# A four-sequence decode kernel: the first queries and scores of its second layer, one key head at a time

## The chip, the cores and the metric

The kernel runs on one core of a Trainium2 chip. The metric is the device time of one execution in microseconds; lower is better.

## What is computed

Two layers over four sequences (B = 4, one new token each, D = 512): attention over a cache of 4096 positions with 32 query heads on 8 key heads of width 128, and a gated feed-forward of width 1792. Both layers use the same weights and the same caches.

```
def _A_ref(x, k_cache, v_cache, wq, wo):
    q = (x @ wq) ...                      # 32 heads of 128
    k, v = repeat(k_cache, 4), repeat(v_cache, 4)
    p = softmax(q . k * Dh ** -0.5)
    return (p . v) @ wo
def _B_ref(x, w_gate, w_up, w_down):
    return (gelu(x @ w_gate) * (x @ w_up)) @ w_down
x = x + _A_ref(layernorm(x), ...)
x = x + _B_ref(layernorm(x), ...)
x = x + _A_ref(layernorm(x), ...)
x = x + _B_ref(layernorm(x), ...)
```

## The kernel before

The work goes sequence by sequence. A key or value head of one sequence is two tiles (`t` = 0 and `NT - 1` = 1, called "last") of 128x2048 bf16, 512 KB each. The keys of one sequence fill SBUF (`KP`, sixteen tiles); each is loaded once, turned in place by VectorE in 32x32 blocks (`Keys.turn`), and serves layer 1 and then layer 2. Values have eight slots (`slots`, `VRing`) and are mostly loaded once for each layer. Key heads stand in two groups of four, `gx` (first in layer 2) and `gy`.

The order of the work is written out by hand, and every engine runs its own instructions in that order. All loads but that of x are issued by SyncE's queue (SP), in the order written, and an issue waits until its target is free.

- `attend_first` does layer 1 of sequence 0, issues the loads of the weights (`load_rest`: wo, w_gate, w_up, and w_down in the parts of `WD_PARTS`), and moves two key tiles, heads 2 and 3 of `gy` at the last t, into four banks of PSUM (`Parked`), so that the first two key tiles of sequence 1 can be loaded into their place at once.
- `dense_first` is the feed-forward of layer 1 for sequence 0. `busy` issues matmuls whose result nobody reads, where TensorE waits for a load.
- Then come the queries of layer 2 for the group `gx`: 64 small matmuls (`q_proj`), rounding on VectorE (`q_round`), sums on TensorE (`q_sums`), and the mask on VectorE that lays them out as weights (`q_spread`, into `qb`).
- `attend(b + 1)` does layer 2 of sequence b together with layer 1 of sequence b + 1. It scores group `gx` (`scores`: for each of four parts `be`, one matmul of 512 columns for each of four heads side by side, in four column strips of the array), loads the keys of the next sequence as tiles come free, takes the softmax (`soft`: maximum, exponential on ScalarE; `soft_turn`), then the same for `gy`; the values of layer 2 follow (`vals2`), then two groups of scores and the values (`vals1`) of layer 1 of the next sequence, whose output goes to `dense`, where the rest of layer 2's values (`prev.fill`) are summed between the steps of the feed-forward.

In `attend`, for the first call alone, the two parked tiles are copied back by ScalarE in four pieces, two before and two after the first softmax:

```
for t in range(NT):
    scores(sc2[0], gx, t)
    if parked and t == 0:
        ...
        parked.back(home, 2)
        ...
        keys.load_pairs(GH // 2 - 1)
    else:
        keys.load_pairs(GH // 2)
before.whole()
p0 = soft(sc2[0], norm)
if parked:
    parked.back(home, 2)
q_build(qy())
```

## Time and profile before

| | |
|---|---|
| Median of three runs | 273.4 us (272.24 to 274.52) |
| Profiled execution | 271.11 us, span 269.2 us, mean granted TensorE clock 0.854 |
| Busy | TensorE 190.0 us, VectorE 174.7, ScalarE 64.2, GpSimd 2.7 |
| Loads | 103.08 MB, mean 383 GB/s |
| Key turns on VectorE (L488) | 64, 1.21 us each |
| Score matmuls (L531) | 512 of 512 columns, 0.45 us each, overlapping |
| Copies back from PSUM on ScalarE (L512, keys) | 4 of 128x1024, 1.01 us each |
| Park copies on VectorE (L500, keys) | 4 of 128x512 words, 0.68 us each, 55.2 to 57.0 us |

All times inside the execution count from the start of the span. In lists of instructions the columns are start, duration, engine, line, operation, what it writes and reads, shape and count; in brackets how long the engine was idle just before and what ended it. A merged row has the duration from its first start to its last end. In tables of stretches the columns are the stretch, its length, the busy time and count of TensorE's matmuls, TensorE's weight loads, VectorE, ScalarE and GpSimd, the granted TensorE clock (1 is full), the share of the DMA engines' time, and GB/s. Lines of the form L123 are those of the kernel before.

### The profile page before, as it was taken

What the parts mean: (1) busy time and instruction counts of PE and PEld (TensorE: products, weight loads), DVE (VectorE), ACT (ScalarE), POOL (GpSimd) and SP (SyncE); (2) the same over time, 40 slices, a digit from 0 to 9 for tenths busy, and PEclk for the clock granted to TensorE, in tenths of its full rate; (3) what the DMA queues carried; (4) which work ended last, traced back from release to release, by engine and by line L of the source; (5) the groups of instructions that cost most, each with busy time, mean ns of one, the idle gap of its engine ahead of it and who ended that gap; (6) DMA issues with size and microseconds to landing.
All of it is one profiled execution on the core that took longest, in us unless ns stands there. A gap on an engine that the chain in (4) does not pass through costs nothing.

```text
span 269.2 us, 8883 instructions
## 1 busy us (share of the span) xinstructions
PE 190.0 (71%) x3943; PEld 113.8 (42%) x3943; DVE 174.7 (65%) x428; ACT 64.2 (24%) x125; POOL 2.7 (1%) x8
## 2 busy tenths in 40 slices
PE   1395255634597896968869969687788786788893
PEld 1333133633364443544426335454354354453561
DVE  3394952130124799875676999566759995768863
ACT  1001000100404412030422610304137113044640
POOL 2000000000000000000000000000000000000001
PEclk9999559555599798687897997889979979799999
DMA  6999999999993999999999999999999999999940
GB/s 244 421 417 421 418 420 416 413 382 402 411 360 100 419 415 418 420 418 416 402 386 417 417 420 417 416 422 416 412 417 415 417 419 417 416 391 386 417 159 3
DMA packets 32430, 103.08 MB, mean 383 GB/s; under 512 B 2692, under 2 KB 8584, under 8 KB 32392
## 3 DMA queue, kind: packets, MB, share of 16 engines
q1 hardware_dynamic: 32368, 102.51, 95.1%
q8 instruction: 31, 0.51, 0.7%
q14 instruction: 7, 0.06, 0.1%
q10 hardware_dynamic: 24, 0.01, 0.0%
HBM read 102.50 MB, written 0.00 MB: 381 GB/s over the span
## 4 chain that ended last, share of the span: by engine, by line
DMA 51%; DVE 21%; PE 17%; SPq 6%; issue 2%; ACT 1%; DVEq 0%; ACTq 0%
DMA v_t<-in_A_v_cache_dram 29%; DMA kp<-in_A_k_cache_dram 13%; DVE kp L488 10%; PE sc L531 7%; DMA wu_sb<-in_B_w_up_dram 5%; DMA kp<-in_A_v_cache_dram 4%; SPq L142 4%; PE so L712 2%; DVE pe L541 2%; DVE q L280 2%; DVE qb L316 1%; PE ot L779 1%; PE y L246 1%; PE q L274 1%; SPq L143 1%
## 5 line engine op out<-in xcount | busy, mean ns | idle before, releaser
L488 DVE STREAM_TRANSPOSE kp<-kp 128x1024 f32<-128x1024 f32 x64 | 74.0, 1206 | 0.2 <-issue 0.2
L531 PE MATMUL sc<-kp,qb 128*32 128x512 bf16 x512 | 66.6, 449 | 7.5 <-DVE qb L316 2.5
L779 PE MATMUL ot<-pe,v_t 128*128 128x32 bf16 x1120 | 35.3, 181 | 14.4 <-DMA v_t<-in_A_v_cache_dram 12.4
L779 PEld LDWEIGHTS <-v_t 128*128 128x128 bf16 x1120 | 33.1, 99 | 24.2 <-DMA v_t<-in_A_v_cache_dram 15.9
L531 PEld LDWEIGHTS <-qb 128*32 128x32 bf16 x512 | 21.3, 102 | 42.2 <-issue 23.1
L553 ACT ACTIVATE pe<-sc,nl 128x512 bf16<-128x512 f32 x8 | 5.5, 687 | 84.9 <-DVE pe L550 67.2
L583 PE MATMUL x<-pe,ident_bf 128*32 128x128 bf16 x192 | 6.0, 255 | 15.1 <-DVE pe L561 15.0
L583 PEld LDWEIGHTS <-ident_bf 128*32 128x32 bf16 x256 | 5.6, 107 | 18.9 <-issue 17.1
L541 DVE TENSOR_REDUCE pe<-sc 128x1 f32<-128x512 f32 x12 | 8.3, 689 | 7.9 <-PE sc L531 7.9
L720 DVE STREAM_TRANSPOSE so<-so 128x256 f32<-128x256 f32 (+1 forms) x19 | 11.1, 584 | 3.2 <-PE so L712 3.1
L712 PE MATMUL so<-v_t,pe 128*32 128x256 bf16 x192 | 10.2, 341 | 2.8 <-ACT pe L586 1.4
L246 PE MATMUL y<-OT_bf,wo_sb 128*128 128x32 bf16 x192 | 7.3, 190 | 6.8 <-DMA wo_sb<-in_A_wo_dram 6.7
L246 PEld LDWEIGHTS <-wo_sb 128*128 128x128 bf16 x256 | 8.6, 102 | 8.0 <-DMA wo_sb<-in_A_wo_dram 7.1
L586 ACT CAST pe<-x 128x512 bf16<-128x512 f32 x12 | 7.0, 585 | 20.3 <-PE x L583 20.3
L712 PE MATMUL so<-v_t,pl 128*32 128x256 bf16 x192 | 9.7, 283 | 2.9 <-DMA v_t<-in_A_v_cache_dram 2.6
L379 DVE TENSOR_TENSOR xb<-XX,y 128x4 bf16<-128x4 f32 (+1 forms) x9 | 1.6, 173 | 14.2 <-PE y L246 14.1
L246 PE MATMUL q<-xb,wq_sb 128*128 128x5 bf16 (+1 forms) x192 | 5.4, 170 | 7.3 <-DMA wq_sb<-in_A_wq_dram 7.3
L561 DVE STREAM_TRANSPOSE pe<-pe 128x512 bf16<-128x512 bf16 x12 | 8.4, 697 | 3.2 <-ACT pe L553 3.2
L616 DVE TENSOR_TENSOR OT_bf<-ot,rden 128x8 bf16<-128x8 f32 (+1 forms) x20 | 3.0, 156 | 11.1 <-PE ot L779 11.0
L360 PE MATMUL yr<-wo_sb,OT_bf 128*2 128x512 bf16 (+1 forms) x96 | 10.2, 494 | 0.0
L310 PE MATMUL qe<-q_bf,ident_bf 128*32 128x16 bf16 x256 | 4.4, 175 | 8.2 <-DVE q_bf L299 6.3
L712 PEld LDWEIGHTS <-pe 128*32 128x32 bf16 x208 | 6.1, 113 | 8.2 <-issue 3.8
(148 smaller groups left out, 229.6 us busy)
## 6 DMA issues: line engine op xcount, KB each, us to landing
v_t<-in_A_v_cache_dram SPq DMA_DIRECT2D x97, 512.0 KB, 8.9
kp<-in_A_k_cache_dram SPq DMA_DIRECT2D x40, 512.0 KB, 12.4
kp<-in_A_k_cache_dram SPq DMA_DIRECT2D x12, 1024.0 KB, 8.3
wq_sb<-in_A_wq_dram SPq DMA_DIRECT2D x2, 2048.0 KB
wo_sb<-in_A_wo_dram SPq DMA_DIRECT2D x4, 1024.0 KB, 11.4
wq_sb<-in_A_v_cache_dram SPq DMA_DIRECT2D x3, 1024.0 KB, 11.2
wg_sb<-in_B_w_gate_dram SPq DMA_DIRECT2D x1, 1792.0 KB
wu_sb<-in_B_w_up_dram SPq DMA_DIRECT2D x1, 1792.0 KB
```

Of the source, the lines that this page charges most:

```text
L142: dq.dma_start(out=wo_sb[:, i * n:(i + 1) * n], in_=wo_dram[:, i * n:(i + 1) * n])
L246: nc.tensor.matmul(dst, lhsT=lhsT, rhs=rhs, start=first, stop=last, skip_group_check=True)
L360: nc.tensor.matmul(self.rows[j:j + x.shape[1]], lhsT=x, rhs=wo_sb[:, i], start=self.n < QD, stop=True, skip_group_check=True)
L488: nc.vector.transpose(out=words, in_=words)
L531: nc.tensor.matmul(sc[s * QS:(s + 1) * QS], lhsT=qb[:, w0:w0 + 2 * W], rhs=kt[:, :, be // 2, :, be % 2], start=(t == 0 and be == 0), stop= ...
L541: nc.vector.tensor_reduce(out=m, in_=sc.rearrange("p c j -> p (c j)"), axis=AX.X, op=ALU.min if norm else ALU.max)
L561: nc.vector.transpose(out=flat, in_=flat)
L583: nc.tensor.matmul(x[a * QS:(a + 1) * QS, s], lhsT=ident_bf[:, s * QS:(s + 1) * QS], rhs=pT[:, a], start=True, stop=True, skip_group_check ...
L586: nc.scalar.copy(out=pe, in_=x.rearrange("p s t c h -> p (s t c h)"))
L712: nc.tensor.matmul(ps[d, :NW * QS], lhsT=x[:, w:w + NW].rearrange("p c h -> p (c h)"), rhs=v[:, i:i + NW, d], start=first and i == 0, stop ...
L720: nc.vector.transpose(out=flat, in_=flat)
L779: nc.tensor.matmul(self.ot[:, s % 2], lhsT=v[:, i, :], rhs=wide(pe[:, s, t * CH + i, :]), start=(done == 0 and i == 0), stop=(done == NT - ...
```

## The change

w_down's last part (three of fourteen row blocks) is loaded in two parts, of two and one. `busy` writes into the bank that is to be used next and no longer into one of its own; six of its matmuls in and after `down` go, two are added ahead of the second group's scores. A dictionary `place` tells where a key tile lies. Three key tiles and not two are parked: the third (head 1 of `gy`, last) goes to one PSUM bank and two SBUF buffers, and three tiles of the next sequence are loaded early. The queries and scores of `gx` for sequence 0 are made in four steps: (head 2, t 0); (3, 0) and (2, last); (3, last), (0, 0) and (1, 0); (0, last) and (1, last). After each step the freed tiles are loaded, one by one, or refilled from what was parked, by ScalarE (three pieces), VectorE (two) and GpSimd (two). The query rows of `gy` and their mask now come before the softmax of `gx`. New functions and the core of the diff:

```diff
-WD_PARTS = (0, 6, 11, 14)
+WD_PARTS = (0, 6, 11, 13, 14)
+WARM = 0
+W_WARM = 64
...
+    place = {(g * GH + s, t): (KP[g][t][s // 2], s % 2)
+             for g in range(NG) for s in range(GH) for t in range(NT)}
+
     def k_tile(i, t):
-        return KP[i // GH][t][i % GH // 2][:, i % 2]
+        pair, n = place[i, t]
+        return pair[:, n]
...
     def q_tile():
         return grp.tile([P, HG], BF16, name="q_bf", tag="q_bf", bufs=1)
-    def q_round(q_bf, q, g, norm):
-        nc.vector.scalar_tensor_tensor(out=q_bf[:], in0=cs_q[:, g], scalar=norm.mean,
+    def q_round(q_bf, q, g, norm, h0=0):
+        own = slice(h0, h0 + q.shape[1])
+        nc.vector.scalar_tensor_tensor(out=q_bf[:, own], in0=cs_q[:, g, own], scalar=norm.mean,
                                        in1=q[:, :, 0], op0=ALU.mult, op1=ALU.subtract)
     def q_build(q):
         q_spread(q_sums(q))
+    def q_sum_tile():
+        return ps_sm.tile([P, GH, BE, rep], FP32, name="qe", tag="sm")
+
     def q_sums(q):
-        qe = ps_sm.tile([P, GH, BE, rep], FP32, name="qe", tag="sm")
+        qe = q_sum_tile()
+        q_sums_of(qe, q, 0, GH)
+        return qe
+
+    def q_sums_of(qe, q, s0, n):
         iv = ident_bf[:].rearrange("p (b w e) -> p b e w", b=NB, e=2)
         for be in range(BE):
             for a in range(QD):
-                nc.tensor.matmul(qe[a * QS:(a + 1) * QS, :, be], lhsT=iv[:, be // 2, be % 2],
-                                 rhs=q, start=True, stop=True, skip_group_check=True)
-        return qe
-
-    def q_spread(qe):
+                nc.tensor.matmul(qe[a * QS:(a + 1) * QS, s0:s0 + n, be], lhsT=iv[:, be // 2, be % 2],
+                                 rhs=q[:, s0 * rep:(s0 + n) * rep], start=True, stop=True,
+                                 skip_group_check=True)
+
+    def q_spread(qe, s0=0, n=GH):
         dst = qb[:, W:].rearrange("p (n x a h) -> p n x a h", x=2, a=QD, h=rep)[:, :, 0]
+        shape = [P, n * BE, QD, rep]
         nc.vector.tensor_tensor(
-            out=dst,
-            in0=qe.rearrange("p s n h -> p (s n) h").unsqueeze(2).broadcast_to([P, NK, QD, rep]),
-            in1=amask.unsqueeze(1).unsqueeze(3).broadcast_to([P, NK, QD, rep]),
+            out=dst[:, s0 * BE:(s0 + n) * BE],
+            in0=qe[:, s0:s0 + n].rearrange("p s n h -> p (s n) h").unsqueeze(2).broadcast_to(shape),
+            in1=amask.unsqueeze(1).unsqueeze(3).broadcast_to(shape),
             op=ALU.mult)
...
-    def busy(count):
...
+    def busy(count, unread, by=None, start=True):
+        rhs = wg_sb[:, 0] if by is None else by
         for _ in range(count):
...
+            nc.tensor.matmul(unread, lhsT=ident_bf[:], rhs=rhs[:, :unread.shape[1]], start=start,
+                             stop=start, skip_group_check=True)
...
-    def down(nb, H_bf):
-        y = acc([KD, WIDE], "y2")
+    def down(nb, H_bf, whole):
+        y = acc([KD, WIDE], "y2", whole)
         for c in range(KF):
-            if c in WD_PARTS[1:]:
-                busy(2)
+            if c == WD_PARTS[1]:
+                busy(1, whole[:, KD * WIDE:], start=False)
             for k in range(KD):
                 mac(y[:, k], wd_sb[:, c, k * P:(k + 1) * P], wide(H_bf[:, c, :]),
...
         def __init__(self, src, homes):
...
+        def back(self, dst, count=1, by=None):
+            for at, part in self.parts[self.n:self.n + count]:
+                to = dst[:, at:at + 2 * part.shape[1]]
+                if by is nc.vector:
                     nc.vector.tensor_scalar(out=to.bitcast(I32), in0=part, scalar1=0, scalar2=None,
                                             op0=ALU.bitwise_or)
+                elif by is nc.gpsimd:
+                    nc.gpsimd.tensor_copy(out=to, in_=part.bitcast(BF16))
                 else:
                     nc.scalar.copy(out=to, in_=part.bitcast(BF16))
...
         vals.step(TG)
         assert vals.left() == 0
         load_rest()
-        busy(0)
-        gx2, gy2 = second_groups[b]
-        parked = Parked(KP[gy2][NT - 1][1].rearrange("p h c d -> p (h c d)"),
-                        [(ps_h, "h"), (ps_x, "x"), (ps_ot[0], "ot"), (ps_ot[1], "ot")])
-        ahead = Keys(b + 1, (gx2, gy2))
-        ahead.load_pairs(1, into=KP[gy2][NT - 1][1])
+        scr = Scratch()
+        early = Early(b + 1, second_groups[b])
         proj = OutProj(o1(b), 1)
         for h in pairs(one(b)):
             proj.heads(h, hp)
         ring.extend(2, b, own)
-        return proj.y, (ahead, parked)
+        return proj.y, early, scr
     ahead_of = [0, 0] + [2] * (B - 2)
+
+    class Early:
+
+
+        def __init__(self, b, groups):
+            self.gx, self.gy = groups
+            last = NT - 1
+            a, c = self.gx * GH, self.gy * GH
+            self.own = dict(place)
+            flat = [k_tile(c + s, last).rearrange("p c d -> p (c d)") for s in range(GH)]
+            self.two = [Parked(flat[2], [(ps_h, "h", 2), (ps_x, "x", 2)]),
+                        Parked(flat[3], [(pool, "ot", 2) for pool in ps_ot])]
+            self.one = Parked(flat[1], [(ps_sc, "sc", 2), (pep, "pe", 4), (pep, "pl", 4, 1)])
+            place[a, 0], place[a + 1, 0] = self.own[c + 2, last], self.own[c + 3, last]
+            place[a + 2, 0] = self.own[c + 1, last]
+            self.keys = Keys(b, groups)
+            self.keys.load_pairs(1)
+            self.keys.load(1)
+
+        def queries(self, b, st):
+            g, n = self.gx, rep
+            norm = Norm(st)
+            q_bf, qe = q_tile(), q_sum_tile()
+
+            def heads(q, s, lo=0, hi=rep):
+                for i in range(lo, hi):
+                    h = s * rep + i
+                    for k in range(KD):
+                        mac(q[:, h % q.shape[1]], wq_sb[g][:, k, h * Dh:(h + 1) * Dh],
+                            wide(xb[:, k, :RUN]), k == 0, k == KD - 1)
+
+            def rounded(q, s):
+                q_round(q_bf, q[:, :, b:b + 1], g, norm, s * rep)
+
+            def masked(s, n):
+                q_spread(qe, s, n)
+
+            q = acc([n, WIDE], "q")
+            heads(q, 2)
+            rounded(q, 2)
+            q = acc([n, WIDE], "q")
+            heads(q, 3, 0, n // 2)
+            q_sums_of(qe, q_bf[:], 2, 1)
+            heads(q, 3, n // 2, n)
+            masked(2, 1)
+            rounded(q, 3)
+            norm.root()
+
+            def second():
+                q_sums_of(qe, q_bf[:], 3, 1)
+                masked(3, 1)
+                self.both = acc([2 * n, WIDE], "q")
+                heads(self.both, 0)
+
+            def third():
+                heads(self.both, 1)
+                rounded(self.both, 0)
+                q_sums_of(qe, q_bf[:], 0, 2)
+                masked(0, 2)
+                norm.scales()
+
+            self.second, self.third = second, third
+            return norm
+
+        def scores(self, sc, qy, norm):
+            gx, gy, own, keys = self.gx, self.gy, self.own, self.keys
+            a, c, last = gx * GH, gy * GH, NT - 1
+
+            def home(i, t, freed):
+                place[i, t] = own[freed]
+                return k_tile(i, t).rearrange("p c d -> p (c d)")
+
+            def load(i, t, freed):
+                home(i, t, freed)
+                assert keys.tile(keys.nl) == (i, t)
+                keys.load(1)
+
+            def first(run):
+                now = {(a + s, t): place[a + s, t] for s, t in run}
+                place.update({k: own[k] for k in now})
+                scores_of(sc, gx, run)
+                place.update(now)
+
+            first([(2, 0)])
+            load(a + 3, 0, (a + 2, 0))
+            self.second()
+            first([(3, 0), (2, last)])
+            load(a, last, (a + 3, 0))
+            load(a + 1, last, (a + 2, last))
+            self.third()
+            q = qy()
+            first([(3, last), (0, 0), (1, 0)])
+            load(a + 2, last, (a + 3, last))
+            to = home(c + 1, last, (a + 1, 0))
+            self.one.back(to, 1, nc.vector)
+            self.one.back(to, 2, nc.gpsimd)
+            self.two[0].back(home(c + 2, last, (a, 0)), 2)
+            first([(0, last), (1, last)])
+            load(a + 3, last, (a, last))
+            to = home(c + 3, last, (a + 1, last))
+            self.two[1].back(to, 1)
+            other = new_scores()
+            qe = q_sums(q)
+            busy(2, other.rearrange("p c j -> p (c j)"))
+            q_spread(qe)
+            self.two[1].back(to, 1, nc.vector)
+            p0 = soft(sc, norm)
+            return p0, other
     def attend(b, qy, before, norm, early=None):
         gx, gy = second_groups[b - 1]
         prob1, prob2 = {}, {}
-        keys, parked = early or (Keys(b, (gx, gy)), None)
+        keys = early.keys if early else Keys(b, (gx, gy))
         turn = keys.turn
         kept2, own2, other2, apart2 = two(b - 1)
         kept1, own1, _, apart1 = two(b)
                        last_bank=lambda: ps_sm.tile([P, 2, WIDE], FP32, name="ot", tag="sm"))
         sc2 = [new_scores(early=True)]
-        for t in range(NT):
-            scores(sc2[0], gx, t)
-            if parked and t == 0:
-                freed = KP[gx][0][0]
-                home = freed.rearrange("p h c d -> p (h c d)")
-                parked.back(home, 2)
-                KP[gx][0][0], KP[gy][NT - 1][1] = KP[gy][NT - 1][1], freed
-                keys.load_pairs(GH // 2 - 1)
-            else:
+        if early:
+            p0, other = early.scores(sc2[0], qy, norm)
+            sc2.append(other)
+        else:
+            for t in range(NT):
+                scores(sc2[0], gx, t)
                 keys.load_pairs(GH // 2)
-        before.whole()
-        p0 = soft(sc2[0], norm)
-        if parked:
-            parked.back(home, 2)
-        q_build(qy())
-        sc2.append(new_scores())
+            before.whole()
+            p0 = soft(sc2[0], norm)
+            q_build(qy())
+            sc2.append(new_scores())
         soft_turn(p0)
-        ready = 2 if parked else 0
+        ready = 2 if early else 0
         turn(ready)
         for t in range(NT):
...
             scores(sc2[1], gy, t)
...
-        g = out_of(0, ffn_in(rhs, wg_sb, "g"))
+        whole = bank("g")
+        busy(WARM, whole[:, :W_WARM], ident_bf)
+        g = out_of(0, ffn_in(rhs, wg_sb, "g", whole))
         sq = gelu(scr, g, shifts(scr, mr, 0), rstd)
-        busy(6)
-        u = ffn_in(rhs, wu_sb, "u")
-        busy(4)
+        whole = bank("u")
+        busy(6, whole[:])
+        u = ffn_in(rhs, wu_sb, "u", whole)
+        whole = bank("y2")
+        busy(4, whole[:])
         u = out_of(1, u)
         H_bf = gate_up(scr, sq, u, shifts(scr, mr, 1), rstd)
-        y = down(nb, H_bf)
-        busy(1)
-        return y
+        return down(nb, H_bf, whole)
...
-    y, early = attend_first()
+    y, early, scr = attend_first()
     prev = NoValues()
     for b in range(B):
-        scr = Scratch()
-        y = dense(b, y, prev, scr) if b else dense_first(y, scr)
+        y = dense(b, y, prev, Scratch()) if b else dense_first(y, scr)
...
         if b == 0:
             ring.pump()
-            norm = Norm(st)
-            norm.root()
-            q = queries(gx)
-            busy(1)
-            q_round(q_bf, q, gx, norm)
-            q_build(q_bf[:])
-            busy(1)
+            norm = early.queries(b, st)

```

## Prediction

> **What bounds the kernel now.** I read the page's slices first. The sixteen DMA engines are busy from start to end but for one hole in slice 13 (80.8 to 87.5 us), and elsewhere the rate stands near 418 GB/s:
>
> ```profile
> DMA  6999999999993999999999999999999999999940
> GB/s 244 421 417 421 418 420 416 413 382 402 411 360 100 419 415 418 420 418 416 402 386 417 417 420 417 416 422 416 412 417 415 417 419 417 416 391 386 417 159 3
> ```
>
> So the stream of loads sets the time, and the hole is what there is to win. The stretches around it give its size (last two columns: DMA share, GB/s):
>
> ```profile
> 78.00:80.00 2.00, 1.96 (x38) 1.09 (x37) 0.21 (x2) 0.00 (x0) 0.00 (x0) 1.00 0.93 375
> 80.00:82.00 2.00, 2.00 (x69) 1.77 (x69) 0.76 (x5) 0.41 (x2) 0.00 (x0) 1.00 0.23 88
> 82.00:84.00 2.00, 1.68 (x38) 0.88 (x41) 0.66 (x4) 0.00 (x0) 0.00 (x0) 1.00 0.00 0
> 84.00:86.00 2.00, 1.91 (x36) 0.86 (x28) 0.85 (x2) 1.86 (x2) 0.00 (x0) 1.00 0.41 57
> 86.00:88.00 2.00, 0.27 (x16) 0.17 (x16) 1.49 (x7) 1.39 (x5) 0.00 (x0) 1.00 0.92 360
> 88.00:90.00 2.00, 1.65 (x16) 0.59 (x20) 2.00 (x4) 1.67 (x2) 0.00 (x0) 0.58 1.02 410
> 90.00:92.00 2.00, 2.00 (x36) 0.82 (x28) 1.16 (x2) 0.00 (x0) 0.00 (x0) 0.57 1.03 424
> ```
>
> Ten microseconds moved 2 x (375 + 88 + 0 + 57 + 360) = 1760 KB where 418 GB/s moves 4180: 2420 KB, or 5.8 us, are lost. The timeline of the DMA queue says why:
>
> ```profile
> 72.44 1.13 SPq L481 DMA_DIRECT2D kp<-in_A_k_cache_dram  x1
> 84.19 2.35 SPq L481 DMA_DIRECT2D kp<-in_A_k_cache_dram  x3
> 90.27 4.58 SPq L472 DMA_DIRECT2D kp<-in_A_k_cache_dram  x8
> ```
>
> After the early pair (72.44) no space for keys is free until the first 16 score matmuls are done (84.17). A load issued into an empty queue reaches full rate late: 5.8 us lost between a stream that would have ended near 80.3 and an issue at 84.2 leave 1.9 us from issue to data. Then the chain that ended last, from these scores on:
>
> ```profile
> 82.99 2.10 PE sc L531 x27
> 85.11 0.70 DVE pe L541
> ...
> 88.35 3.67 PE sc L531 x27
> 92.04 0.69 DVE pl L541
> ```
>
> It is a chain of compute, which from 92.04 on runs through VectorE almost without a gap (sixteen key turns of 1.13 us from start to start, three softmaxes) to the last softmax of the next attention at 114.41 and its reciprocal at 118.31. **Two clocks run side by side**, the stream and this VectorE chain, and they meet at the next dense stage: its values are waited for by TensorE, but only briefly:
>
> ```profile
> 122.97 0.40 PE L712 MATMUL so<-v_t,pe 128*32 128x256 bf16 x8 [0.24 <-DMA v_t<-in_A_v_cache_dram]
> 124.23 0.57 PE L779 MATMUL ot<-pe,v_t 128*128 128x32 bf16 x16 [0.64 <-DMA v_t<-in_A_v_cache_dram]
> 125.46 0.58 PE L779 MATMUL ot<-pe,v_t 128*128 128x32 bf16 x16 [0.16 <-DMA v_t<-in_A_v_cache_dram]
> ```
>
> 0.24 + 0.64 + 0.16 = 1.04 us, and a wait of 0.3 at 120.5: **the VectorE chain is only 1.0 to 1.4 us (I take 1.2) ahead of the stream there**. The change must be counted on both clocks.
>
> **The stream's side.** Last part of w_down in two: the last bytes land when they did (79.20), 4 matmuls follow and not 12; at 0.026 us apart that is 0.2 us earlier. The extra issue waits in a full ring (the three before took 1.1 to 6.7 us), which the data ahead of it hide: even 3 us later the pair would be issued at 75.5, and its data start near 77.8. The six fillers taken out lie in waits for w_down or for VectorE, and the two new ones ahead of the second scores in the wait for their mask: nothing, if the clock holds (below). Three more park copies on VectorE (0.68 and two halves, between 0.17 and 0.68 each): VectorE is idle from 57.7 to the layer norm, nothing. The third tile early is 524 KB: 1.25 us more data.
>
> First key step, from rows: y at 79.52, residual and statistics as before, 0.2 earlier (79.77); 16 query matmuls and not 64 end at 80.43; rounding 80.45; sums 0.28 later (82.17 - 81.89) at 80.73; mask 0.34 later (82.51 - 82.17) at 81.07. A mask of 64 elements isn't shown: between the smallest VectorE row, 0.14, and the 0.42 of 256 elements; by elements 0.22. Scores start at 81.35. One head alone issues 4 matmuls in a row, 0.215 apart at the full clock (heads one by one at 101.74 to 102.78), as long as four heads side by side. So the first load is issued at 82.5, not 84.19: 1.7 us earlier. The hole: 5.8 - 1.25 - 1.7 = 2.85 us.
>
> The next steps: scores of (3,0),(2,last) 82.84 to 83.95 and two issues at 84.0 and 84.4; then query rows for the other group (16 matmuls, 0.9) put the third scores at 85.7 to 86.8, issue 86.9; the fourth 86.6 to 87.7, issue 87.8; the next four tiles at 89.5. Each of the first tiles lasts only 1.25 us, so the stream may run dry for 0 to 0.4 at the second, the fourth and the sixth: 0 to 0.9. **The stream gains 2.0 to 2.9 us.**
>
> **VectorE's side.** Scores of the first group are done at 87.7 where they were at 85.09: four serial steps instead of eight rounds back to back. Only then can its softmax start, and three pieces of work now stand ahead of it on VectorE: one restored piece of 0.68 (86.9, hidden by the scores), the mask of the other group (87.84 to 88.26) and the last restored piece (0.59 to the next start). The reduce starts at 88.8 and not 85.11. From there the old rows: 1.2 to the maximum, 0.33 to the exponential, 0.81 to the turn of the probabilities (91.15), 0.62, two key turns of 1.13: the second softmax begins at 94.0. Before, 92.04: **2.0 us later**. What hid some of it: before, VectorE was idle from 91.16 to 92.04, while TensorE ran the second scores at half clock. Bounds: 1.1 (the restored piece and the masks cost nothing, every step 0.1 shorter) to 3.5 (each serial step 0.3 longer, 0.68 in full). ScalarE's three restoring copies (0.91 apart from 86.8, done 89.6) precede the exponential at 90.3 and are hidden; 0.7 us more and they are not. The second scores need them too: they end near 90.9, 3 us before their softmax's turn.
>
> GpSimd copies two pieces of 128x512, which the trace doesn't show there. Bounds from its rows: 0.2 (a memset of 128 columns) to 1.2 each (four times the 0.29 of the affine select). I take 1.0; they start at 86.8 and are harmless until 92.8, that is 3 us each. The Trainium skill's page "GPSIMD Engine Reference", 3.1, gives some 1.8 cycles an element at best; an estimate of 0.8 us from it would leave the sum as it is. No run so far shows it.
>
> **Where they meet.** From 92 to 118 nothing on VectorE waits for data, so all 2.0 us arrive at the reciprocal (118.31 to 120.3). The first refill behind it waits for the parking copies there:
>
> ```profile
> SPq L634 <- DVE park L500: 12.0, 6, 3.6
> ```
>
> That load (119.81) was issued some 2.0 us before the stream needed it (data to 123.67, less 1.9). Issued 2.0 later, its data begin where they did before: the 2.0 to 2.9 us gained at the hole are given back here. The layer's output comes 2.0 - 1.2 = 0.8 us later, with it the next refills of the dense stage (127.49, 129.60), which the stream already waited for (402 and 386 GB/s in slices 20 and 21). A wait of 0.26 at 133.23 takes up part. Net: **+0.8 - 0.2 = +0.6 us**. On the profiled execution (span 269.2, time 271.1) that is 271.7; its time lies 2.3 below the median of the runs, 273.4, so I forecast **274.0** as median. With the bounds of the delay, 1.1 to 3.5, the sum is -0.3 to +2.1: 273.1 to 275.5.
>
> **Rivals.** (1) *The hole's gain stays.* It needs the VectorE chain not to be late at all: a delay under zero. For it: the page puts 51% of the chain on DMA and stretches of 10 us end on a landing. Against it: the slices at 20 and 21, where the stream itself waits, and the order written out, in which the softmax comes last. Price: -2.85 at most, 270.6; 0.12.
>
> (2) *The clock falls in the new stage*, the other side. The stretch 86 to 88 with TensorE busy for 0.27 of 2.0 us is followed by a granted clock of 0.58 and 0.57. The change takes out six fillers and puts VectorE between its steps. If a stretch falls to about half busy, the four steps of serial matmuls cost twice: 16 x 0.215 = 3.4, and the query rows 0.9: 4.3 us more on VectorE's delay, 0.6 + 4.3 = +4.9: 278.3. Against it: by my times TensorE is busy for over 85% of 78 to 88. The Trainium skill, "TensorE: Matmul & The Clock Gate", Part 1, has the clock halved after an idle window of some 3.4 us; by that rule this is unlikely, and the second scores would run at full clock (2.0 and not 3.67 us), which shortens nothing, since VectorE is later. Chance 0.13.
>
> (3) *Restoring is what is late*: GpSimd's copies at 4.5 us each (its one arithmetic row, 1.02 us for 4 columns, shows that it can be slow), or ScalarE's and VectorE's copies pushed behind them. Then the second scores end near 97 and their softmax starts 5 late: +3.8 - 0.2 = +3.6, 277.0. It decides from 3 us a copy. Chance 0.22.
>
> That the third tile isn't early (its issue held by the park) changes the hole by 1.25 and not the sum, as the stream isn't last.
>
> **Numbers.** Forecast 0.53, within 1% of no change (2.7 us; the three runs spread over 0.8%, about what can be told). Range: 271.0, where half of rival 1 is taken in, to 277.6, which takes in rival 3 and leaves out most of rival 2. The likeliest's own range is 273.1 to 275.5. Faster by over 1%: rival 1, 0.12; slower by over 1%: rivals 2 and 3, 0.35; the rest 0.53.
>
> **What would show it.** The hole: a first single-tile issue near 82.5 and some 2 to 3 us less lost by 92. The first softmax's reduce at 88.8, the second's at 94.0, the reciprocal after the last softmax near 120. A refill after the parking copies near 121.8, and slices 20 and 21 no fuller than before. I am wrong if the second softmax starts at or before 92, or if the stream after 118 runs ahead of what it did by the whole gain.

## The result, and the profile after

The changed kernel takes **275.6 us** (median of 16 runs, 273.2 to 279.4) against 273.9 for the kernel before in the same session (16 runs, 270.7 to 276.5). The ratio is **1.0083, 95% interval 1.0055 to 1.011**: about 0.8% slower, 1.5 to 3.0 us. Its profiled execution took 276.25 us, span 274.5. The profile of before is of a quick execution (271.1, 2.7 below this median), so the 5.1 us between the two profiles overstate the difference; below, places in the traces are compared with places, and times with times. A ratio here compares the runs of each kernel that lie within 1.5% of its quickest, and the traces shown below are of such runs but for those of a_turn and a_order.

The slices of the page after (DMA: busy share; GB/s), and the first line of its chain:

```profile
DMA  7999999999996899999999999999999999999920
GB/s 257 420 418 420 417 420 417 406 383 409 403 347 229 296 408 418 414 393 324 400 330 370 416 420 417 417 421 411 407 417 417 417 418 418 411 383 405 419 107 3
...
DMA 37%; DVE 31%; PE 21%; SPq 6%; issue 3%; ACT 1%; DVEq 0%; ACTq 0%
```

The hole is no longer empty (229 GB/s in its slice, not 100), but the slices around it are thin (347, 296), and new thin ones are the 19th, 21st and 22nd (324, 330, 370), where before there were 416, 386 and 417. DMA has gone from 51% of the chain to 37%, VectorE from 21% to 31%.

For the whole story one quantity is useful, the **stream's lag**: time since the start less the bytes moved so far divided by 418 GB/s. Read from the DMA records of both traces it is 4.0 us at 78 before and 3.8 after; **9.8 and 10.1 at 98; 10.6 and 14.7 at 150**. So the hole cost as much as before, and 4.6 us were lost between 98 and 150, where the kernel before lost 0.8. Each of these lags is of one execution.

The stretches of the first key steps, after (the columns as in the table of before: busy PE, PEld, DVE, ACT, POOL, then granted clock, DMA share, GB/s):

```profile
80.00:82.00 2.00, 1.84 (x60) 1.50 (x62) 1.13 (x7) 0.00 (x0) 0.00 (x0) 1.00 0.65 258
82.00:84.00 2.00, 2.00 (x35) 1.19 (x34) 0.29 (x2) 0.41 (x2) 0.00 (x0) 0.53 0.11 37
84.00:86.00 2.00, 1.89 (x24) 0.75 (x21) 0.08 (x1) 0.00 (x0) 0.00 (x0) 0.62 0.67 246
86.00:88.00 2.00, 1.80 (x44) 1.03 (x45) 1.16 (x5) 0.00 (x0) 0.00 (x0) 1.00 0.81 272
88.00:90.00 2.00, 1.70 (x35) 0.86 (x32) 1.60 (x5) 1.67 (x2) 1.17 (x2) 1.00 0.96 338
90.00:92.00 2.00, 1.98 (x32) 0.66 (x28) 1.69 (x6) 1.34 (x3) 0.00 (x0) 1.00 0.88 293
92.00:94.00 2.00, 0.78 (x23) 0.40 (x19) 1.27 (x2) 1.05 (x4) 0.00 (x0) 1.00 0.84 291
94.00:96.00 2.00, 1.19 (x34) 1.09 (x35) 2.00 (x3) 0.54 (x1) 0.00 (x0) 0.94 0.84 332
```

Two things are to be seen. The clock stands at 0.53 and 0.62 from 82 to 86, where the kernel before had 1.00. And from 86 to 96 the stream runs, but at 272 to 338 GB/s; up to 91 it is fed one tile at a time. VectorE's part in the same place, from its timeline (start, duration); the last line is that of the kernel before:

```profile
88.36 0.69 DVE L530 TENSOR_SCALAR kp<-park 128x512 int32<-128x512 int32 x1
89.42 0.42 DVE L332 TENSOR_TENSOR qb<-qe,masks 128x256 bf16<-128x256 f32 x1 [0.36 <-PE qe L325]
89.76 0.68 DVE L530 TENSOR_SCALAR kp<-park 128x512 int32<-128x512 int32 x1
90.36 0.68 DVE L567 TENSOR_REDUCE pe<-sc 128x1 f32<-128x512 f32 x1
...
93.37 2.33 DVE L507 STREAM_TRANSPOSE kp<-kp 128x1024 f32<-128x1024 f32 x2
95.62 0.65 DVE L567 TENSOR_REDUCE pl<-sc 128x1 f32<-128x512 f32 x1
...
121.87 2.44 DVE L520 TENSOR_SCALAR park<-v_t 128x512 int32<-128x512 int32 x4
...
118.48 2.45 DVE L500 TENSOR_SCALAR park<-v_t 128x512 int32<-128x512 int32 x4
```

The first softmax's reduce comes at 90.36 (85.11 before), the second's at 95.62 (92.04), the parking copies at 121.87 (118.48). VectorE is 3.6 us late at the second softmax, and 3.4 of it are still there at the parking copies. The first refill of a parked buffer follows its copy at once: it is issued at 123.19, 1.32 us after the first copy starts, and before the change at 119.81, 1.33 us after it. What these late refills do to the stream, in the next stretches:

```profile
126.00:130.00 4.00, 3.68 (x101) 2.62 (x96) 2.23 (x8) 0.59 (x1) 0.00 (x0) 0.94 0.91 296
130.00:134.00 4.00, 2.99 (x108) 1.94 (x104) 3.21 (x12) 3.19 (x5) 0.00 (x0) 1.00 1.05 402
134.00:138.00 4.00, 2.21 (x48) 1.12 (x40) 0.93 (x5) 0.00 (x0) 0.00 (x0) 0.84 0.99 385
138.00:142.00 4.00, 3.31 (x68) 1.37 (x64) 2.90 (x11) 0.41 (x2) 0.00 (x0) 0.73 0.98 345
142.00:146.00 4.00, 1.95 (x48) 0.91 (x40) 2.61 (x9) 1.18 (x3) 0.00 (x0) 1.00 0.94 309
```

Before, these five moved 415, 392, 377, 404 and 420 GB/s; the first, fourth and fifth of them:

```profile
126.00:130.00 4.00, 3.86 (x74) 2.16 (x74) 1.97 (x9) 1.69 (x3) 0.00 (x0) 0.59 1.02 415
...
138.00:142.00 4.00, 1.85 (x48) 0.85 (x40) 2.85 (x9) 1.18 (x3) 0.00 (x0) 1.00 1.01 404
142.00:146.00 4.00, 3.85 (x63) 2.15 (x56) 1.49 (x5) 0.58 (x1) 0.00 (x0) 0.62 1.03 420
```

### The profile page after: what moved, and what is told of

Read it like the earlier page. It is cut to its first block, busy times and chain, and to the rows that moved or that the text cites. A ratio compares the mean times of both kernels' runs of the same rounds, so it can differ in the third digit from the quotient of the medians.

```text
span 274.5 us, 8969 instructions
## 1 busy us (share of the span) xinstructions
PE 194.2 (71%) x3968; PEld 116.6 (42%) x3971; DVE 177.3 (65%) x437; ACT 63.5 (23%) x124; POOL 3.9 (1%) x10
## 4 chain that ended last, share of the span: by engine, by line
DMA 37%; DVE 31%; PE 21%; SPq 6%; issue 3%; ACT 1%; DVEq 0%; ACTq 0%
DMA v_t<-in_A_v_cache_dram 18%; DVE kp L507 17%; DMA kp<-in_A_k_cache_dram 9%; PE sc L557 8%; DMA wd_sb<-in_B_w_down_dram 6%; DMA kp<-in_A_v_cache_dram 4%; SPq L149 4%; PE ot L805 2%; DVE pe L567 2%; PE so L738 2%; PE q L281 2%; DVE qb L332 2%; PE y L253 1%; DVE q L287 1%; DVE pe L587 1%
## 5 line engine op out<-in xcount | busy, mean ns | idle before, releaser
L557 PE MATMUL sc<-kp,qb 128*32 128x512 bf16 x512 | 69.1, 455 | 6.6 <-DVE kp L507 2.1
L805 PE MATMUL ot<-pe,v_t 128*128 128x32 bf16 x1120 | 35.0, 181 | 13.7 <-DMA v_t<-in_A_v_cache_dram 12.0
L557 PEld LDWEIGHTS <-qb 128*32 128x32 bf16 x512 | 22.8, 103 | 41.0 <-issue 23.1
L746 DVE STREAM_TRANSPOSE so<-so 128x256 f32<-128x256 f32 (+1 forms) x19 | 11.1, 584 | 2.1 <-PE so L738 1.8
L738 PE MATMUL so<-v_t,pe 128*32 128x256 bf16 x192 | 10.1, 341 | 2.2 <-ACT pe L612 0.9
L325 PE MATMUL qe<-q_bf,ident_bf 128*32 128x16 bf16 (+2 forms) x288 | 6.0, 175 | 7.7 <-DVE q_bf L307 4.9
L642 DVE TENSOR_TENSOR OT_bf<-ot,rden 128x8 bf16<-128x8 f32 (+1 forms) x20 | 3.0, 155 | 11.1 <-PE ot L805 11.1
L376 PE MATMUL yr<-wo_sb,OT_bf 128*2 128x512 bf16 (+1 forms) x96 | 9.6, 467 | 0.0
L287 DVE STREAM_TRANSPOSE q<-q 128x512 f32<-128x512 f32 x7 | 5.1, 730 | 6.7 <-PE q L281 6.7
## 6 DMA issues: line engine op xcount, KB each, us to landing
wq_sb<-in_A_v_cache_dram SPq DMA_DIRECT2D x3, 1024.0 KB, 11.2
wg_sb<-in_B_w_gate_dram SPq DMA_DIRECT2D x1, 1792.0 KB, 12.4
```

Source lines behind the costliest of these rows:

```text
L287: nc.vector.transpose(out=flat, in_=flat)
L376: nc.tensor.matmul(self.rows[j:j + x.shape[1]], lhsT=x, rhs=wo_sb[:, i], start=self.n < QD, stop=True, skip_group_check=True)
L557: nc.tensor.matmul(sc[s * QS:(s + 1) * QS], lhsT=qb[:, w0:w0 + 2 * W], rhs=kt[:, :, be // 2, :, be % 2], start=(t == 0 and be == 0), stop= ...
L738: nc.tensor.matmul(ps[d, :NW * QS], lhsT=x[:, w:w + NW].rearrange("p c h -> p (c h)"), rhs=v[:, i:i + NW, d], start=first and i == 0, stop ...
L746: nc.vector.transpose(out=flat, in_=flat)
L805: nc.tensor.matmul(self.ot[:, s % 2], lhsT=v[:, i, :], rhs=wide(pe[:, s, t * CH + i, :]), start=(done == 0 and i == 0), stop=(done == NT - ...
```

## The experiments

**Theory A**: VectorE's delay decides. The stream's place at 98 does not matter, because the refills from 118 on wait for parking copies at the end of VectorE's chain. **Rival C**: the stream's own feeding between 82 and 96 decides, and VectorE has slack. **Rival B**: the clock, by the fillers taken out, is the cause of all of it. (In the expectations of a_fillers and b_no_fillers the letters stand otherwise: A there is that the clock fell because the fillers went, B that the fillers don't matter.) "Lost by 150" in an expectation is the lag at 150. Ratios are to the kernel before, run beside each on the same chip.

| kernel | first parking copy | lag at 98 | lag at 150 | half clock between 78 and 92 | ratio (95%) |
|---|---|---|---|---|---|
| before | 118.5 | 9.8 | 10.6 | 88.3-91.7 | 1 |
| b_no_fillers | 119.0 | 11.1 | 11.9 | 82.3-85.7 | 1.005 (1.001-1.008) |
| b_warm | 118.1 | 10.1 | 10.2 | none | 1.003 (0.999-1.007) |
| b_turn | 117.9 | 9.9 | 11.2 | none | 0.999 (0.994-1.003) |
| b_late | 120.9 | 9.8 | 13.1 | none | 1.014 (1.009-1.019) |
| after | 121.9 | 10.1 | 14.7 | 82.1-85.5 | 1.008 (1.006-1.011) |
| a_fillers | 121.2 | 8.9 | 12.8 | none | 1.009 (1.005-1.013) |
| a_soft_first | 121.2 | 10.3 | 12.4 | 81.4-84.8 | 1.005 (1.002-1.008) |
| a_two_tiles | 120.7 | 9.3 | 13.7 | none | 1.013 (1.008-1.019) |
| a_wd3 | 122.1 | 9.4 | 12.9 | 81.5-84.9 | 1.010 (1.007-1.014) |
| a_order | 121.0 | 9.9 | 14.1 | none | 1.012 (1.006-1.017) |
| a_turn | 120.4 | 9.1 | 11.3 | 81.0-84.4 | see below |
| a_best | 119.1 | 9.3 | 9.6 | none | 0.999 (0.995-1.003) |
| a_best2 | 118.8 | 8.1 | 9.6 | none | 1.001 (0.997-1.004) |

The trace's columns are of one execution each; run to run a kernel's time spreads over 1 to 3%. Nor is the lag the whole span: at 200 us b_warm's is 11.0 and that of before 10.7, yet b_warm's traced execution is 4.1 us longer (273.3 and 269.2). So the lag says where the stream loses, and the ratio what the kernel loses.

### The clock: a_fillers and b_no_fillers

```diff
# a_fillers: the changed kernel, and
-            if c == WD_PARTS[1]:
-                busy(1, whole[:, KD * WIDE:], start=False)
+            if c in WD_PARTS[1:]:
+                busy(2, spare[:])
...
+        busy(1, spare[:])          # behind the down sums
+            busy(1, t3[:, n * WIDE:])   # between the second head's queries
# b_no_fillers: the kernel before, and
-            if c in WD_PARTS[1:]:
-                busy(2)
+            if c == WD_PARTS[1]:
+                busy(1)
...
-        busy(1)                    # behind the down sums, ahead of and behind the masks
```

> The changed kernel with fillers put back: two matmuls of 512 columns ahead of each later part of w_down, one after the last, one of 384 columns between the queries of head 3. Theory A (the clock fell from 82.1 to 85.5 us because the fillers went, and what this adds on VectorE's chain is paid in full): granted clock 1.0 from 78 to 88, first key step's load issued near 82.5, second softmax of sequence 0 on VectorE starting near 94.2 instead of 95.6, time about 1.003 of before instead of 1.0083. Rival B (the clock fell by the chance of where its windows lie, the fillers don't matter): clock again at half in 82 to 86 in about as many runs, ratio 1.007 to 1.010. Rival C (the stream of loads decides, not VectorE): the loads come 1.4 us earlier too, but the stream is still fed one tile at a time; ratio 1.005 to 1.008.

> The kernel before with the six fillers taken out as the change does (one left ahead of the second part of w_down). Theory A: the clock falls in 78 to 88 us here too, the 32 first scores take up to 3.7 us instead of 2.1, the second softmax starts 1.0 to 2.0 us later than 92.0, time 1.003 to 1.007 of before. Rival B: clock and time as before, ratio 0.998 to 1.002.

In both the clock did what the fillers let it: full from 78 to 92 in a_fillers, halved from 82.3 to 85.7 in b_no_fillers. The table says the same: of the six traces without the fillers five have a half clock that begins between 81.0 and 82.3, and of the eight with them none has one there. In b_no_fillers that is 1.3 us of lag at 98 and half a microsecond on VectorE, and the interval of its ratio, 1.001 to 1.008, lies above 1. So the six fillers are worth about 1.3 us (0.4 to 2.3) in the kernel before, and to cost their removal at nothing was right only on its condition. In a_fillers VectorE was 0.7 us earlier and the lag 1.2 us smaller at 98; but the time, 1.009, did not fall, and the 1.003 that was expected lies outside its interval. Rival B is out as the whole cause: with the clock full the changed kernel is still slower, and its parking copies are still 2.7 us late.

### VectorE's order: a_soft_first

```diff
-            q_spread(qe)
-            self.two[1].back(to, 1, nc.vector)
             p0 = soft(sc, norm)
+            q_spread(qe)
+            self.two[1].back(to, 1, nc.vector)
```

> The changed kernel with the softmax of the first group ahead of the other group's mask and of the last restored piece on VectorE. Theory A (VectorE's chain decides): the softmax's reduce starts 0.9 to 1.0 us earlier, the second softmax near 94.7 instead of 95.6, time 1.004 to 1.006 of before. Rival C (the stream decides): the second scores and with them the next eight key loads come 1.2 to 1.4 us later, the stream has lost that much more by 100 us, time 1.010 to 1.014.

Second softmax at 94.94 (0.7 earlier), lag at 98 10.3 (no better), at 150 12.4 (2.3 better), ratio 1.005 (1.002 to 1.008). This is as theory A has it, and the interval excludes what rival C expected (1.010 to 1.014). That the kernel became faster than the changed one (1.008) is not shown: the two intervals overlap.

### A delay on VectorE alone: b_late

```diff
# the kernel before, second softmax of the first batch
-        nc.vector.tensor_reduce(out=m, ...)
+        for _ in range(1 + late):      # late = 5 there
+            nc.vector.tensor_reduce(out=m, ...)
```

> The kernel before with one edit: the first reduce of the second softmax is done six times over instead of once (same operands, same result), so VectorE comes some 3.0 to 3.4 us later out of that softmax, about what the change costs it (3.6 us), and nothing of the stream of loads, the first key step or the fillers is touched. Theory A (VectorE's delay decides: the refills behind the parking copies go out late): the first parking copy goes from 118.5 to 121.5-121.9, the stream, which has lost 9.8 us by 100 as before, has lost 12.5 to 14 by 150 instead of 10.6; ratio 1.006 to 1.010. Rival C (what decides is the stream's own loss between 86 and 100, tile by tile; VectorE has the slack): lost by 150 stays at 10.6 to 11; ratio 0.999 to 1.003.

This is the cleanest of the runs: nothing of the change is in it. Its VectorE timeline and the stretches after the parking copies:

```profile
91.03 4.28 DVE L542 TENSOR_REDUCE pl<-sc 128x1 f32<-128x512 f32 x6
...
120.91 2.45 DVE L500 TENSOR_SCALAR park<-v_t 128x512 int32<-128x512 int32 x4
```

```profile
126.00:130.00 4.00, 3.59 (x102) 2.69 (x103) 2.17 (x11) 0.99 (x4) 0.00 (x0) 1.00 0.96 356
...
138.00:142.00 4.00, 3.28 (x80) 1.46 (x71) 2.99 (x12) 0.41 (x2) 0.00 (x0) 0.98 0.91 328
142.00:146.00 4.00, 1.82 (x40) 0.73 (x36) 2.82 (x9) 1.18 (x3) 0.00 (x0) 0.88 1.01 349
```

The copies come 2.4 us late (less than forecast: in this execution the second softmax could start 1.0 earlier than in the profile of before). The lag is untouched at 98 (9.8) and 13.1 at 150, with the thin stretches of the changed kernel (356, 328, 349 here; 296, 345, 309 there). Here too the first refill is issued 1.33 us after the first copy (122.24). The time rose by 0.9 to 1.9%, more than the 0.6 to 1.0 expected; in this trace another 2.7 us are lost between 158 and 200, where the changed kernel lost 0.3 and the kernel before 0.1. C is out: a delay on VectorE of less than the change's, with the stream untouched up to 98, makes the kernel as slow as the change does.

### Taking the delay back: a_turn, a_best, b_turn

In the changed kernel VectorE is busy for 0.08 of the 2 us from 84 to 86, with small masks and roundings around them. The turn of the first early key tile can stand there.

```diff
# a_turn: the changed kernel, and
             self.second()
+            keys.turn()
             first([(3, 0), (2, last)])
...
-        turn(ready)
+        turn(ready - 1 if early else 0)
# a_best: a_turn + a_fillers + a_soft_first
# b_turn: the kernel before with b_warm's seven fillers, and turn(1) ahead of the first softmax
```

> The changed kernel with one edit: the turn of the first early key tile on VectorE stands between the second key head's mask and the rounding of the next queries, in idle time of VectorE (83.8 to 87), and not after the first softmax. Theory A: VectorE's chain is 1.1 us earlier than in the changed kernel (second softmax near 94.5 instead of 95.6, first parking copy near 120.7 instead of 121.9), lost by 100 as in it (10), lost by 150 some 13 instead of 14.7; ratio 1.003 to 1.006 where the changed kernel had 1.008. Rival C: the stream's feeding is untouched, so the time is that of the changed kernel, 1.007 to 1.011.

> The changed kernel with three edits together: the fillers on TensorE of a_fillers, the softmax ahead of mask and restored piece as in a_soft_first, and the early key turn of a_turn. Theory A: second softmax near 93.2 (94.9 with the fillers alone, less 0.6 and 1.1), still 1.2 later than before the change; first parking copy near 119.5; lost by 100 near 9.0, by 150 near 11; ratio 0.999 to 1.003. Rival C (the stream alone): 0.9 us less lost by 100 than before the change, all of it kept: 0.996 to 0.998.

> The kernel before with the seven fillers of b_warm after the query rows of the second group, and with one early key turn on VectorE ahead of the first softmax, in the idle time from 83.4 to 85.5 in which it waits for scores. VectorE's chain comes up to 1.1 us earlier than in b_warm (second softmax near 90.9, where the second scores end, instead of 91.5; first parking copy near 117.2 instead of 118.1). Theory A: the refills are no longer late at all, so lost by 150 stays at what is lost by 100 (10.1), and only the 0.8 us that the kernel before lost there can be won: 0.996 to 0.999. Rival C: as b_warm, 1.000 to 1.004.

In a_turn the copies came at 120.4 and the lag at 150 fell by 3.3 us, 1.0 of it at 98. Its time can't be used: its runs lie between 270.2 and 279.1 with a median of 275.3 (273.0 before), and its ratio, 0.998 (0.993 to 1.003), rests on the few near that one quick run.

In **a_best** all of it comes together:

```profile
83.22 1.24 DVE L509 STREAM_TRANSPOSE kp<-kp 128x1024 f32<-128x1024 f32 x1
...
92.81 0.66 DVE L569 TENSOR_REDUCE pl<-sc 128x1 f32<-128x512 f32 x1
...
119.06 2.45 DVE L522 TENSOR_SCALAR park<-v_t 128x512 int32<-128x512 int32 x4
```

```profile
126.00:130.00 4.00, 3.17 (x80) 1.95 (x81) 2.65 (x11) 2.33 (x5) 0.00 (x0) 1.00 1.03 419
...
138.00:142.00 4.00, 1.79 (x40) 0.66 (x36) 3.06 (x9) 1.18 (x3) 0.00 (x0) 0.83 1.03 413
142.00:146.00 4.00, 3.62 (x71) 1.96 (x64) 1.29 (x5) 0.59 (x1) 0.00 (x0) 0.74 1.02 413
```

The turn stands at 83.22, the copies at 119.06, the thin stretches are gone, and the lag at 150 is 9.6, 1.0 below the kernel before. The time is that of the kernel before (0.995 to 1.003), about 1% below the changed kernel. The 1.0 us at 150 was not kept: this execution lost 1.8 us between 158 and 200, where the kernel before lost 0.1, with a half clock from 181.6 to 185.0 in its next dense stage.

b_turn is the same from the other side: VectorE 0.6 earlier than in the kernel before, nothing gained in time. It also missed what theory A expected of the stream: its lag at 150 was 11.2, where 10.1 was expected. So the theory holds in one direction: VectorE later than in the kernel before costs time, VectorE earlier was not seen to win any.

### The parts: a_two_tiles and a_wd3

```diff
# a_two_tiles
-            self.one = Parked(flat[1], ...)
-            place[a + 2, 0] = self.own[c + 1, last]
-            self.keys.load(1)
# ... and the loads behind it moved up by one freed place, the restoring of self.one gone
# a_wd3
-WD_PARTS = (0, 6, 11, 13, 14)
+WD_PARTS = (0, 6, 11, 14)
```

> The changed kernel without its third early key tile: three parked pieces and their restoring (VectorE 0.68, GpSimd two copies) are gone, the first freed place takes head 2's tile. What is tested is what the 524 KB of early data are worth. Theory A (VectorE's chain decides the refills from 118 on, the stream's place at 100 does not): 1.25 us more lost by 90 than in the changed kernel (near 9.6 instead of 8.3), but VectorE 0.6 earlier for the missing restored piece (second softmax 95.0, first parking copy 121.3), so lost by 150 14 to 15, as in it; ratio 1.005 to 1.009. Rival C (the stream decides): the 1.25 us stay: lost by 150 near 16, ratio 1.011 to 1.014.

> The changed kernel with w_down's last part whole again (three parts instead of four). The prediction gave the split 0.2 us: 4 matmuls instead of 12 after the last bytes. Theory A (the last bytes land later when they are a load of their own, so the split gains nothing): the last matmul of the down sums at 79.6 to 79.8 as in the changed kernel (79.70), ratio as the changed kernel's, 1.005 to 1.011. Rival (the split is worth its 0.2 us): it ends at 79.9 to 80.0; the ratio can't tell 0.2 us.

a_two_tiles had the full clock without fillers (more on that at the end), and with it shows the key steps as the prediction drew them: issues at 82.46, 84.00, 84.44, 86.91, 87.73 and 89.49. Its VectorE lines:

```profile
88.87 0.68 DVE L567 TENSOR_REDUCE pe<-sc 128x1 f32<-128x512 f32 x1
...
94.19 0.65 DVE L567 TENSOR_REDUCE pl<-sc 128x1 f32<-128x512 f32 x1
```

Of the third tile's 1.25 us of cover (the time its 524 KB keep the stream busy) 0.4 is left at 98: lag 9.3 here, 8.9 in a_fillers, which has the tile and the full clock; its issues are 0.7 later for the fillers, so the tile itself is worth 0.4 to 1.1. Its lag at 150 went as A had it; its ratio lies above A's range and in C's, but with an interval that reaches down to 1.008 it decides nothing.

In a_wd3 the last matmul of the down sums ends at 79.91, in the changed kernel at 79.69, which by itself is what the rival expected. But the stream of a_wd3 was 0.28 us later at 78, and still its whole last part landed at 79.40, the split one of the changed kernel at 79.38. Set against the stream, the split gained nothing.

### Further tries: b_warm, a_order, a_best2

```diff
# b_warm
             q_raw = q_rows(b, g)
+            if b == 0:
+                busy(7)
# a_order: a_best, and
             first([(2, 0)])
             load(a + 3, 0, (a + 2, 0))
+            first([(2, last)])
+            load(a, last, (a + 2, last))
             self.second()
...
-            scores(sc2[1], gy, t)
-            keys.load(GH)
+            for s in range(GH):
+                scores_of(sc2[1], gy, [(s, t)])
+                keys.load(1)
# a_best2: a_best with q_spread ahead of soft again and WD_PARTS = (0, 6, 11, 14)
```

> The kernel before with seven fillers on TensorE after the query rows of the second group (85.7 to 87.3 us), where it waits for VectorE. Theory A: the second scores run at full clock, 2.0 us instead of 3.7, the second softmax starts at 91.2 instead of 92.0, all of VectorE's chain after it 0.9 us earlier, time 0.996 to 0.998 of before. Rival C (the stream decides): the stream isn't dry at that point, time 0.999 to 1.001.

> a_best with another order of the key steps, to feed the stream: head 2's two tiles one after the other, then head 3's, and the other group's first four heads one by one, each load issued as soon as its tile is free; the mask of the other group ahead of the softmax again (the restored piece stays behind it). No work is added. Issues near 82.9, 83.8, 85.7, 86.6 instead of 82.9, 84.5, 84.9, 87.4. Theory A together with the stream's own loss: lost by 100 8.0 to 8.6 instead of 9.3; VectorE's chain as in a_best or 0.3 later (first parking copy 119.1 to 119.5), so of the 0.7 to 1.3 us the larger part is kept: lost by 150 8.3 to 9.2; ratio 0.994 to 0.998. Rival (VectorE's 0.6 us on top of the kernel before still decide, the stream only waits longer at the refills): lost by 150 9.6 or more, ratio 0.998 to 1.002.

> a_best with two edits that should hand the stream something at no cost to VectorE's chain: the other group's mask ahead of the softmax again (its scores, and the loads behind them, start some 0.5 us earlier; the restored piece stays behind the softmax, in the wait for the exponential), and w_down's last part whole (the split gained nothing). Theory A: second softmax 92.8 to 93.3, first parking copy 119.1 to 119.6 (118.5 before the change, 121.9 with it), lost by 100 near 8.9 instead of 9.3, by 150 at most 10; ratio 0.995 to 1.000, which would be below both kernels if its interval excludes 1. Rival (where VectorE is 0.6 us later than before the change, it is still what decides): lost by 150 10.5 to 11.5; ratio 1.000 to 1.004.

b_warm did in its place what was meant (full clock, copies 0.4 earlier, lag at 150 10.2), and the time missed: the interval, 0.999 to 1.007, leaves out the gain that theory A expected (0.996 to 0.998).

**a_order** was a plain miss. That "no work is added" was wrong. TensorE's lines of the scores in a_best, then in a_order:

```profile
83.39 1.04 PE L559 MATMUL sc<-kp,qb 128*32 128x512 bf16 x8
...
90.07 2.00 PE L559 MATMUL sc<-kp,qb 128*32 128x512 bf16 x32 [1.27 <-DVE qb L332]
```

```profile
84.42 1.91 PE L559 MATMUL sc<-kp,qb 128*32 128x512 bf16 x8
...
90.77 3.00 PE L559 MATMUL sc<-kp,qb 128*32 128x512 bf16 x32
```

Eight matmuls on two heads, side by side in two column strips, take 1.04 us; eight on the two tiles of one head, in one strip, 1.91. All eight tiles of the other group take 2.00 against 3.00. The Trainium skill, "TensorE: Matmul & The Clock Gate", Part 3, says that matmuls in different 32-column tiles of the array run at the same time; the trace agrees. The query rows behind these scores begin 1.9 us later (87.25 against 85.35), the mask stands ahead of the softmax again, and the first softmax came 2.4 us later (90.64 against 88.23), the copies at 121.0, and although the lag at 90 was the smallest of the runs then at hand (7.5), it was 14.1 at 150: theory A once more, against my own purpose.

a_best2 fed the stream better without touching VectorE: lag 8.1 at 98, 1.7 below the kernel before, copies only 0.3 later. By 150 it was 9.6, as in a_best: 1.6 us given back from 118 on. The lag is what theory A expected; the ratio, 1.001 (0.997 to 1.004), fits the rival as well. No version was measurably quicker than the kernel before.

## Why the prediction was right, and where not

The time lies in the range, and the kernel is slower by about 0.8% for the reason given: two clocks, VectorE's late, the stream's part without weight. But +0.6 us were forecast and +2.3 (1.5 to 3.0) measured, and 275.6 is just above the likeliest case's own range (273.1 to 275.5, or -0.3 to +2.1). The term that was too small is VectorE's delay: 2.0 us forecast, 3.6 measured, which is outside its bounds (1.1 to 3.5). With 3.6 in its place the forecast's own sum gives 3.6 - 1.2 - 0.2 = +2.2. So the path was right and the size was not, and that the time still fell in the range is in part luck: its upper end had been set for rival 3, which did not come.

- **The meeting of the two clocks**: shown, by b_late above all. A first parking copy up to 119.1 goes with 0.1 to 1.6 us lost between 98 and 150, one from 120.4 on with 2.1 to 4.6, and the lag at 98 tells nothing of it. The first refill was forecast at 121.8 and went out at 123.19, as late as VectorE. The slack was rightly sized: VectorE 3.4 late, less 1.2, makes 2.2, and the refill of 127.49 went out at 129.67. (Of the 1.2, the wait of 0.3 at 120.5 stands in no row as a wait for data: the weight load at 120.51 had been idle for 0.17.) What the step left out is the second turn of the wheel: the stream is thin from 126 to 130, and the next key load went from 137.61 to 141.88, 4.3 us late. That the values delivered late are what held it is argued and was not tested.
- **VectorE's delay, 2.0 us**: the steps were right, their condition was not. With the full clock (a_two_tiles) the reduce comes at 88.87 where 88.8 was forecast and the second softmax at 94.19 for 94.0. In the changed kernel they come 1.5 and 1.4 later, because the second step's scores ran at half clock (83.48 to 85.37) and each later issue went out 1.4 to 1.5 us late.
- **The clock (rival 2, 0.13)**: the step that failed, and what made the delay too small: by the comparison with a_two_tiles 1.4 of the missing 1.6 us. "By my times TensorE is busy for over 85% of 78 to 88" was about true and no protection: 2.95 of 3.41 us are 86%.

```profile
78.70:82.11 3.41, 2.95 (x90) 2.33 (x87) 1.44 (x8) 0.00 (x0) 0.00 (x0) 1.00 0.78 316
82.11:85.52 3.41, 3.41 (x46) 1.49 (x41) 0.22 (x1) 0.41 (x2) 0.00 (x0) 0.50 0.43 157
```

These are two neighbouring windows of the trace's clock records, the one ahead of the fall and the one in it. The Trainium skill, "TensorE: Matmul & The Clock Gate", Part 1, has the clock halved after an idle window; by that rule it should have stayed, and here the measurement decides. The rival's price was too high, though: 4.3 us were counted for all four steps, while one window of 3.41 us fell, and the steps behind it came 1.4 later than in a_two_tiles. So its time, 278.3, did not come.

- **The stream's gain, 2.0 to 2.9 us**: failed. The lag rose by 6.3 us from 78 to 98, before by 5.8. The later issues are one part. The other is the thin stream between the tiles: 0 to 0.9 us were allowed for, and at the full clock of a_fillers, where issues are 0.7 late, the stretch still took 4.9 us of lag instead of 2.9 to 3.8. What makes it thin is only in part the spacing of the issues (see the end). That the gain did not matter was the forecast's own argument, so the miss hardly moved the sum.
- **The third tile**, 1.25 us of cover: 0.4 to 1.1. **The split of w_down**, 0.2: nothing.
- **Restoring** (rival 3): two GpSimd copies took 0.61 us each, not 1.0; ScalarE's three stood from 88.33 to 91.17 and held the other group's second scores, but those were over (92.3) before VectorE came to them at 95.62. VectorE's first piece was hidden and its second cost its 0.6.
- **The hole's gain stays** (rival 1): a_best comes nearest to it, and shows why not: even with VectorE only 0.6 late the gain of 1.0 at 150 did not reach the end.

What stays open is where the 1.0 us of a_best went. Its trace shows a half clock in the next dense stage and a lag that grows there, and so does that of a_best2 (half clock from 181.0 to 184.4, 1.5 us lost between 158 and 200). All six traces with a half clock that lasts beyond 184 there lost 1.5 to 2.7 us; of the other eight six lost 0.1 to 0.8, but a_fillers lost 1.2 and a_two_tiles 1.9. That the clock is the cause was not tested.

## What to carry to other kernels

Where a transfer waits for a buffer that another engine empties at the end of a long chain, time won for the transfers earlier is only a loan; look first for what the next refill waits on, and count a delay on that engine in full, less the slack that the stream leaves it (here 3.6 less 1.2). Before splitting a step into serial parts, see whose idle time the parts open (here VectorE's, 83 to 88), and move later work of the same engine into it: one key turn, a softmax moved up and the fillers, together, took back the whole loss. A filler is not idle work to be costed at nothing: price its removal by the clock it holds.

## What the runs showed of the hardware

**The clock's fall depends also on where its windows lie.** In each trace the half-clock stretches sit on a grid of 3.41 us, and the grid lies differently in each execution. The kernel before and b_late run the same instructions up to 91, with 0.27 us of TensorE work between 86 and 88; before fell at 88.3, b_late did not. The Trainium skill, "TensorE: Matmul & The Clock Gate", Part 1, calls the window free-running, and the traces agree. How near the edge the changed kernel runs is seen in a_two_tiles, the same steps in a window that lies 0.3 us later against them:

```profile
78.80:82.21 3.41, 2.91 (x82) 2.17 (x80) 1.44 (x8) 0.20 (x1) 0.00 (x0) 1.00 0.43 176
82.21:85.62 3.41, 3.10 (x81) 2.00 (x79) 0.86 (x5) 0.20 (x1) 0.00 (x0) 1.00 0.59 169
```

Busy for 2.91 us it stayed, where 2.95 fell. In b_late it even stayed after a window that was busy for 2.31 us:

```profile
87.00:90.42 3.42, 2.31 (x52) 1.07 (x56) 2.98 (x6) 2.59 (x5) 0.00 (x0) 1.00 1.02 404
90.42:93.83 3.41, 1.82 (x55) 1.62 (x48) 3.31 (x5) 0.59 (x1) 0.00 (x0) 1.00 1.03 423
```

So the busy time of the records does not decide it. Four 512-column score matmuls start in the first window of a_two_tiles (81.39 to 82.05), in that of the changed kernel three (81.55 to 81.99; the fourth at 82.29). It may be the columns that stream; what counts was not tried. How many executions of the changed kernel lost the clock there isn't known: the spread of its runs (2.2%) doesn't tell, as that of the kernel before is as wide (2.1%).

**After a gap, a stream fed tile by tile ran thin for longer than its issues explain.** From 82.95 to 90.98 the changed kernel issued tiles of 512 KB 0.4 to 2.5 us apart, five in 8.0 us, which is 326 GB/s. From 91.41 to 95.77 it issued seven, twice what 418 GB/s moves in that time. Still the stream moved only 291 GB/s from 92 to 94 and 332 from 94 to 96, with the DMA engines busy for 0.84 of the time; in the kernel before, which fed it with pairs of tiles up to 86, they were busy for 1.01 from 94 to 96 and moved 416. What holds the stream there is open.
